# Parts of two feed-forward groups begun inside the attention of batch 0, with norms, key tiles and loads re-ordered

## The chip, the core and the metric

The kernel runs on one core of a Trainium2 chip. The metric is the device time of one execution in microseconds; lower is better. TensorE (PE in the profile) does the matrix products, VectorE (DVE) and ScalarE (ACT) the elementwise work, GpSimd (POOL) the squares and the transfers that cast, SyncE (SP) issues most other transfers.

## The reference

Two stages, one feeding the other. First, cosine attention: 8 batches of 12 heads, 448 positions, head size 64. Then a feed-forward layer on 3584 tokens: 768 to 2048, leaky ReLU with slope 0.01, 2048 to 768.

```python
q_n = q / (np.linalg.norm(q, axis=-1, keepdims=True) + 1e-06)
k_n = k / (np.linalg.norm(k, axis=-1, keepdims=True) + 1e-06)
scores = np.matmul(q_n, k_n.transpose(0, 1, 3, 2)) / tau
scores = scores - np.max(scores, axis=-1, keepdims=True)
attn = np.exp(scores)
attn = attn / (np.sum(attn, axis=-1, keepdims=True) + 1e-09)
x = np.matmul(attn, v)            # then heads side by side: (3584, 768)
h = x @ w_in
out = np.maximum(0.01 * h, h) @ w_out
```

## The kernel before

The order of work on every engine is the order of the program text: the kernel is written under a manual schedule, and each engine and each queue takes its instructions in that order, waiting where an input or a buffer is not ready.

Heads go in pairs: pair `s` (0 to 47) has two heads, six pairs to a batch. Two pairs make a group of four heads, `j` (0 to 23), three groups to a batch. The 448 positions are three tiles of 128 and a rest of 64; the rests of two heads share one tile.

For each pair: `load_qk(s)` brings q and k on SyncE (four transfers: q main, k main, and the two rests); the buffers rotate among four pairs, so a load waits until the pair four before it is normalised and squared. `squares(s)` (L163, GpSimd) and `sums(s)` (L174, VectorE) and `roots(s)` (L181 to 183, ScalarE) and `normalise(s)` (L191 and L195, VectorE) give the normalised heads `qn`. `hold(...)` (L426) is a tiny GpSimd copy that makes GpSimd wait for `qn`. `transposes(s)` turns them: for pairs below 12 on TensorE (L209) with a VectorE copy (L233), from pair 12 on with a transposing transfer on SyncE (L227). `scores(s, ...)` or `key_tiles` gives the score tiles (L252, TensorE) and their exponentials (L264, ScalarE).

For each group: `totals(j)` sums the exponentials with matmuls by ones (L275) and inverts the sum on ScalarE (L286, L287, tile `rb`); `products(j, e)` multiplies with the values (L275): twelve matmuls on `v_b(j)`, then four on the rest tiles `v_rem` of the batch; `scale(j, e)` (L306, VectorE) writes two of the six rows of `xT`. `attend(j)` is all of these for one group. `load_v(j)` and `load_v_rem(b)` bring the values on GpSimd's queue.

Feed-forward: tokens go in chunks `c`, 384 and 512 columns in turn. `first(c, m)` (L324) is one of 16 groups of six matmuls over the six rows of `xT`, with a Prelu on ScalarE (L330); `second(c, ts, half)` (L349) is 16 matmuls over `hT` and one half of `w_out`, with a copy on VectorE (L360) and the store. `load_w_in(i)` brings a quarter of `w_in` (half the columns, every second row), `load_w_out(half)` half the columns of `w_out`, on GpSimd's queue.

Three stages follow each other. (1) A loop over the six pairs of batch 0: attention only; `fill(2)` puts two idle matmuls on a tile `warm` (L417) into TensorE's order where it would wait. (2) Straight code around pairs 6 and 7: group 2, and the first 13 groups `first(0, m)` in hand-written places. (3) A loop over batches 1 to 7 by units; each unit has an attention part, one pair's norms, and as many feed-forward groups from a queue as a plan of costs (`ATTEND`, `BLOCK`) gives it.

Accumulators lie in eight banks. `banks(count, keep)` deals the free bank that has been unused longest; `keep` holds a bank until `given_back`. In stage 1 pairs of banks (scores) come from 0 to 3 and single ones from 4 to 7.

Of the kernel before, what the change touches and what calls it, by code (L numbers as in the profile page):

```python
# [10 lines left out]
AF = mybir.ActivationFunctionType  # L11
# [5 lines left out]
def kernel(  # L17
# [10 lines left out]
    nc = tc.nc  # L28
# [15 lines left out]
    WARM = 22  # L44
    ATTEND = 5500
    BLOCK = 1800
    assert REM == 64 and D == 64

    ctx.enter_context(tc.manual_schedule())
# [23 lines left out]
    kept = {}  # L73
    deals = {"n": 0, "apart": True}

    def banks(count, keep=None):
        lo, hi = (0, 8) if not deals["apart"] else (0, 4) if count == 2 else (4, 8)
        x = min(
            (i for i in range(lo, hi, count) if not set(range(i, i + count)) & set(kept.values())),
            key=lambda i: max(age[i : i + count]),  # L80
        )
        deals["n"] += 1
        age[x : x + count] = [deals["n"]] * count
        if keep:
            kept[keep] = x
        return ps[:, x] if count == 1 else ps[:, x : x + count]

    def given_back(keep):
        deals["n"] += 1
        age[kept.pop(keep)] = deals["n"]  # L90
# [12 lines left out]
    def load_w_in(i):  # L103
        n0, e = i // 2 * (D_ff // 2), i % 2
        gp.dma_start(
            out=w_in_sb[:, e::2, n0 : n0 + D_ff // 2], in_=w_in_r[e, :, :, n0 : n0 + D_ff // 2]
        )

    def load_w_out(half):
        n0 = half * HALF  # L110
        gp.dma_start(out=w_out_sb[:, :, n0 : n0 + HALF], in_=w_out_r[:, :, n0 : n0 + HALF])
# [42 lines left out]
    def squares(s, engs=(gp, gp)):  # L154
        if s >= NSLOT:
            return
        tiles = []
        for x, eng, name in zip(raw[s], engs, ("sq0", "sq1")):
            sq = sqp.tile(list(x.shape), F32, name=name)
            if eng is nc.scalar:  # L160
                nc.scalar.activation(sq, x, func=AF.Square)
            else:
                eng.tensor_tensor(sq, x, x, op=ALU.mult)  # L163
            tiles.append(sq)
        sqs[s] = tiles
# [12 lines left out]
    def roots(s):  # L178
        if s >= NSLOT:
            return  # L180
        nc.scalar.activation(ss[s], ss[s], func=AF.Ln, bias=tiny)  # L181
        nc.scalar.activation(ss[s], ss[s], func=AF.Exp, scale=0.5)
        nc.scalar.activation(ss[s], ss[s], func=AF.Identity, bias=eps)  # L183
# [3 lines left out]
    def normalise(s):  # L187
        if s >= NSLOT:
            return
        r = smp.tile([128, 14], F32, name="r")  # L190
        nc.vector.reciprocal(r, ss[s])  # L191
        qn[s] = qnp.tile([128, 7, 2, D], BF16, name="qn")
        for x, lo, hi, r0 in ((raw[s][0], 0, 4, 0), (raw[s][1], 4, 7, 8)):
            nt = hi - lo
            nc.vector.tensor_tensor(  # L195
                qn[s][:, lo:hi],
                x.rearrange("p h t d -> p t h d"),
                r[:, r0 : r0 + 2 * nt].rearrange("p (h t) -> p t h", h=2)
                .unsqueeze(3).to_broadcast([128, nt, 2, D]),
                op=ALU.mult,  # L200
            )
# [35 lines left out]
    def scores(s, kis):  # L237
        key_tiles([(s, ki) for ki in kis])
# [43 lines left out]
    def totals(j):  # L282
        sm = banks(1)
        strip_products(j, sm, lambda g, ki: ones, lambda g: ones_rem[:, g // 2])
        rb = rbp.tile([128, S], F32, name="rb")
        nc.scalar.activation(rb, sm[:, :S], func=AF.Ln)  # L286
        nc.scalar.activation(rb, rb, func=AF.Exp, scale=-1.0)  # L287
        rbs[j] = rb
# [3 lines left out]
    def products(j, e, po=None):  # L292
        b, jj = divmod(j, NQ)
        if po is None:
            po = banks(1, (j, e))
        pos[j, e] = po
        vm = vb[j].rearrange("p h t (d e) -> p h t e d", e=2)
        vr = vrb[b % 2].rearrange("p j g (d e) -> p j g e d", e=2)
        strip_products(j, po, lambda g, ki: vm[:, g, ki, e], lambda g: vr[:, jj, g, e])
# [15 lines left out]
    def chunk_cols(c):  # L315
        return (0, MAIN) if c % 2 == 0 else (MAIN, 512)

    def first(c, m):
        c0, n = chunk_cols(c)
        if m == 0:  # L320
            hT[c] = htp.tile([128, MT, 512], BF16, name="hT")
        pm = banks(1)
        for kt in range(KT):
            nc.tensor.matmul(  # L324
                out=pm[:, :n],
                lhsT=w_in_sb[:, kt, m * 128 : (m + 1) * 128],
                rhs=xT[c // 2][:, kt, c0 : c0 + n],
                start=(kt == 0), stop=(kt == KT - 1),
            )
        nc.scalar.activation(out=hT[c][:, m, :n], in_=pm[:, :n], func=AF.Prelu, alpha=0.01)  # L330

    osb = {}

# [43 lines left out]
    work = {}  # L377
    for c in range(B):
        c0, n = chunk_cols(c)
        groups = [(KT * n, lambda c=c, m=m: first(c, m)) for m in range(MT)]  # L380
        order = [(ts, half) for half in range(2) for ts in range(n // 128)] if c == 0 else [
            (ts, half) for ts in range(n // 128) for half in range(2)
        ]
        work[c] = groups + [
            (MT * HALF, lambda c=c, ts=ts, half=half: second(c, ts, half)) for ts, half in order
        ]
# [27 lines left out]
    def fill(count):  # L414
        wm = banks(1)
        for i in range(count):
            nc.tensor.matmul(  # L417
                out=wm, lhsT=warm[:, :128], rhs=warm, start=(i == 0), stop=(i == count - 1)
            )
# [34 lines left out]
    for s in range(NPAIR):  # L454
        j = s // 2 - 1 if s >= 2 else None
        even = s % 2 == 0
        n = s + 2 if s + 2 <= NPAIR else None
        scores(s, (0,))
        if s == 1:
            roots(2)  # L460
        if j is not None and not even:
            products(j, 1)
        scores(s, (1,))
        fill(2)
        if s and n:
            sums(n, (0,))
        normalise(s + 1)
        load_qk(s + 5)
        if j is not None and not even:
            scale(j, 0)  # L470
        hold(qn[s + 1][:, 6, 0, 0:1])
        squares(s + 3)
        if not even:
            load_v(s // 2 + 1)
        if s != 1 and s < 5:
            load_w_in(max(s - 1, 0))
        if s == 5:
            load_v_rem(1)
        if n:
            sums(n, (1,))  # L480
        scores(s, (2,))
        if not even:
            fill(2)
            scores(s, (3,))
        transposes(s + 1)
        if s == 0:
            sums(2, (0,))
        if not even:
            fill(2)
        if n and s:  # L490
            roots(n)
        if j is not None and not even:
            scale(j, 1)
        if j is not None and even:
            totals(j)
            products(j, 0)

    def attend(j):
# [4 lines left out]
        for e in range(2):  # L503
            scale(j, e)

    def norms(s):
        roots(s)
        normalise(s)
        if s >= DMA_FROM:
            transposes(s)  # L510
        load_qk(s + 4)


    deals["apart"] = False
    s, j = NPAIR, NQ - 1
# [1 line left out]
    scores(s, (0, 1))  # L517
    sums(s + 1)
    feed_groups(0, 1)
    norms(s + 1)  # L520
    load_w_out(0)
    hold(qn[s + 1][:, 6, 0, 0:1])
    squares(s + 3)
    sums(s + 2)
# [14 lines left out]
    feed_groups(0, 2)  # L539
    scores(s + 1, (1, 2))  # L540
    normalise(s + 3)
    load_qk(s + 7)
    feed_groups(0, 1)
    transposes(s + 2)
    sums(s + 4)
# [1 line left out]
    roots(s + 4)  # L547
    scores(s + 1, (3,))
    normalise(s + 4)
    load_qk(s + 8)  # L550
    hold(qn[s + 4][:, 6, 0, 0:1])
    squares(s + 5)
    feed_groups(0, 1)
# [24 lines left out]
    for b in range(1, B):  # L578
        queue += work[b - 1]
        units = opened if b == 1 else whole  # L580
        costs = [BLOCK + (ATTEND if at is not None else 0) for at, _, _ in units[1:] + [(2, 0, 0)]]
        for i, (at, tiles, ahead) in enumerate(units):
            share = (sum(g[0] for g in queue[:-1]) + sum(costs[i:])) / (len(units) - i) - costs[i]
            if b > 1 and i == 0:
                at = -1
            if at is not None:
                attend(b * NQ + at)
                load_v(b * NQ + at + 2)
            key_tiles([(b * NPAIR + p, ki) for p, ki in tiles])
            done = 0  # L590
            if b == 1 and i < 2:

                if i == 1:
                    cost, fn = queue.pop(0)
                    fn()
                    done += cost
                transposes(NPAIR + 4 + i)
            if ahead and b * NPAIR + ahead < NSLOT:
                s = b * NPAIR + ahead
                sums(s)  # L600
                norms(s)
                hold(qn[s][:, 6, 0, 0:1])
                squares(s + 1)
            if at == 1:
                load_v_rem(b + 1)
            while len(queue) > 1 and (i == len(units) - 1 or done + queue[0][0] / 2 <= share):
                cost, fn = queue.pop(0)
                fn()
                done += cost
# [38 lines left out]
```

## Time and profile before

| | |
|---|---|
| median of 3 runs | 430.74 us (430.70 to 430.92) |
| the profiled execution | 430.73 us |
| its span, first to last instruction | 428.7 us |
| TensorE busy | 417.2 us, 97% of the span |
| ScalarE, VectorE, GpSimd busy | 267.5, 186.5, 137.0 us |
| granted TensorE clock | 0.998 |
| bytes moved | 53.65 MB, mean 125 GB/s |

In the span TensorE does, by groups of instructions: second feed-forward product 151.9 us, first 150.9 us, scores 46.5 us, products and totals 79.7 us, and 15.6 us of warm-up and fill matmuls. Matmuls are pipelined, so a group's time by the timeline is more than what the chain of waits gives it; where a duration is needed to add up, the chain's is used.

Read a timeline line as: start, duration, engine, source line, operation, output <- inputs, shape, count, and in brackets how long the engine sat idle before it and what released it. Read a wait line as: engine and line that waited, what it waited for, microseconds in total, times, longest. In lines on queues the figures are packets, megabytes and share of the 16 engines' time; "DMA to landing" runs from the issue until the data are there.

### The profile page before, as it was taken

What the parts mean: (1) busy time and instruction counts of PE and PEld (TensorE: products, weight loads), DVE (VectorE), ACT (ScalarE), POOL (GpSimd) and SP (SyncE); (2) the same over time, 40 slices, a digit from 0 to 9 for tenths busy, and PEclk for the clock granted to TensorE, in tenths of its full rate; (3) what the DMA queues carried; (4) which work ended last, traced back from release to release, by engine and by line L of the source; (5) the groups of instructions that cost most, each with busy time, mean ns of one, the idle gap of its engine ahead of it and who ended that gap; (6) DMA issues with size and microseconds to landing.
All of it is one profiled execution on the core that took longest, in us unless ns stands there. A gap on an engine that the chain in (4) does not pass through costs nothing.

```text
span 428.7 us, 8667 instructions
## 1 busy us (share of the span) xinstructions
PE 417.2 (97%) x3333; PEld 208.9 (49%) x3333; DVE 186.5 (44%) x366; ACT 267.5 (62%) x494; POOL 137.0 (32%) x208
## 2 busy tenths in 40 slices
PE   8699999999999999999999999999999999999995
PEld 3234554544455555544455555544455555554563
DVE  5775756643453545343353444552444441220021
ACT  4997886677753886577663786658745596434300
POOL 4676542714124143612324132631334110000000
PEclk9999999999999999999999999999999999999999
DMA  7999999964558355953748456865447422010032
GB/s 173 193 230 220 217 224 210 195 166 92 121 120 169 97 120 104 221 100 90 128 98 161 105 127 134 170 105 142 86 99 152 72 64 41 38 73 2 0 75 73
DMA packets 102888, 53.65 MB, mean 125 GB/s; under 512 B 68928, under 2 KB 97856, under 8 KB 102848
## 3 DMA queue, kind: packets, MB, share of 16 engines
q1 hardware_dynamic: 77296, 40.98, 39.1%
q0 software_dynamic: 25056, 11.80, 21.9%
q8 instruction: 26, 0.43, 0.4%
q10 hardware_dynamic: 496, 0.33, 0.2%
q14 instruction: 14, 0.11, 0.1%
HBM read 45.61 MB, written 11.01 MB: 132 GB/s over the span
## 4 chain that ended last, share of the span: by engine, by line
PE 91%; DVE 4%; ACT 1%; DMA 1%; SPq 1%; issue 1%; POOL 1%; DVEq 0%; POOLq 0%
PE ps L324 34%; PE ps L349 33%; PE ps L275 13%; PE ps L252 9%; DVE qn L195 2%; DMA q_h<-in_q_dram 1%; PE ps L209 1%; DVE ss L174 1%; POOL sq L163 1%; PE ps L417 1%; SPq L127 0%; DVE r L191 0%; ACT ss L183 0%; DVE qkT L233 0%; DVE osb L360 0%
## 5 line engine op out<-in xcount | busy, mean ns | idle before, releaser
L349 PE MATMUL ps<-w_out_sb,hT 128*128 128x384 bf16 x896 | 151.9, 326 | 0.2 <-DVE xT L306 0.2
L264 ACT ACTIVATE pe<-ps 128x896 bf16<-128x896 f32 x144 | 122.5, 918 | 46.2 <-PE ps L252 44.5
L324 PE MATMUL ps<-xT,w_in_sb 128*128 128x384 bf16 (+1 forms) x768 | 150.9, 353 | 0.0
L349 PEld LDWEIGHTS <-hT 128*128 128x128 bf16 x896 | 85.3, 98 | 64.1 <-issue 9.6
L324 PEld LDWEIGHTS <-w_in_sb 128*128 128x128 bf16 x768 | 73.1, 98 | 72.4 <-issue 7.0
L330 ACT ACTIVATE hT<-ps 128x384 bf16<-128x384 f32 (+1 forms) x128 | 65.1, 540 | 40.5 <-PE ps L324 40.1
L426 POOL CAST seen<-qn 128x1 f32<-128x1 bf16 x47 | 8.6, 182 | 209.7 <-DVE qn L195 209.7
L360 DVE COPY osb<-ps 128x384 f32<-128x384 f32 (+1 forms) x56 | 30.9, 552 | 99.3 <-PE ps L349 86.9
L174 DVE TENSOR_REDUCE ss<-sq 128x8 f32<-128x512 f32 (+1 forms) x96 | 56.7, 613 | 17.8 <-POOL sq L163 15.7
L252 PE MATMUL ps<-qkT 64*128 64x448 bf16 (+1 forms) x384 | 46.5, 358 | 4.9 <-ACT pe L264 2.9
L163 POOL TENSOR_TENSOR sq<-q_h 128x512 f32<-128x512 f32 x46 | 47.7, 1036 | 2.4 <-DMA q_h<-in_k_dram 1.6
L191 DVE RECIPROCAL r<-ss 128x14 f32<-128x14 f32 x48 | 11.6, 241 | 82.5 <-ACT ss L183 82.5
L306 DVE TENSOR_TENSOR xT<-ps,rb 128x448 bf16<-128x448 f32 x48 | 27.9, 619 | 30.1 <-ACT rb L287 30.1
L163 POOL TENSOR_TENSOR sq<-k_h 128x384 f32<-128x384 f32 x46 | 37.7, 820 | 0.0
L275 PE MATMUL ps<-pe,v_b 128*32 128x448 bf16 x576 | 35.6, 353 | 0.0
L286 ACT ACTIVATE rb<-ps 128x448 f32<-128x448 f32 x24 | 13.0, 541 | 34.5 <-PE ps L275 34.5
L195 DVE TENSOR_TENSOR qn<-q_h,r 128x512 bf16<-128x512 f32 x48 | 33.4, 697 | 1.9 <-DVE r L191 0.3
L252 PEld LDWEIGHTS <-qkT 64*128 64x128 bf16 (+1 forms) x384 | 13.0, 96 | 38.6 <-issue 31.8
L195 DVE TENSOR_TENSOR qn<-k_h,r 128x384 bf16<-128x384 f32 x48 | 26.5, 551 | 0.0
L264 ACT ACTIVATE pr<-ps 128x896 bf16<-128x896 f32 x24 | 22.3, 927 | 0.0
L275 PEld LDWEIGHTS <-v_b 128*32 128x32 bf16 x576 | 15.2, 97 | 11.9 <-issue 0.4
L150 POOL DMA_DIRECT2D v_rem<-in_v_dram x32 | 20.4, 643 | 0.1
(39 smaller groups left out, 183.5 us busy)
## 6 DMA issues: line engine op xcount, KB each, us to landing
q_h<-in_q_dram SPq DMA_DIRECT2D x48, 192.0 KB, 3.2
k_h<-in_k_dram SPq DMA_DIRECT2D x47, 192.0 KB, 3.2
out_dram<-osb SPq DMA_DIRECT2D x30, 192.0 KB, 3.3
v_b<-in_v_dram POOLq DMA_DIRECT2D x24, 192.0 KB, 5.1
out_dram<-osb SPq DMA_DIRECT2D x12, 384.0 KB, 2.9
w_in_sb<-in_moe_w_in_dram POOLq DMA_DIRECT2D x4, 768.0 KB, 9.8
w_out_sb<-in_moe_w_out_dram POOLq DMA_DIRECT2D x2, 1536.0 KB, 21.0
q_h<-in_q_dram SPq DMA_DIRECT2D x48, 32.0 KB, 3.8
```

Of the source, the lines that this page charges most:

```text
L150: gp.dma_start(out=vrb[b % 2][lo : lo + 64, :, g], in_=r[g])
L163: eng.tensor_tensor(sq, x, x, op=ALU.mult)
L174: nc.vector.tensor_reduce(o.rearrange("p (h t) -> p h t", h=2), sqs[s][i], axis=AX.X, op=ALU.add)
L195: nc.vector.tensor_tensor(qn[s][:, lo:hi], x.rearrange("p h t d -> p t h d"), r[:, r0 : r0 + 2 * nt].rearrange("p (h t) -> p t h", h=2) .u ...
L252: nc.tensor.matmul(out=out[:, a, :S], lhsT=x[rows, c0:c1], rhs=x[rows, 0:S], start=True, stop=True,)
L264: nc.scalar.activation(out=dst, in_=sc[:, :, :S], func=AF.Exp, scale=inv_tau)
L275: nc.tensor.matmul(out=x[32 * g : 32 * g + 32, :S], lhsT=weights(g, ki) if ki < 3 else rem(g), rhs=pe[s][:, ki, a, :] if ki < 3 else pr[j] ...
L306: nc.vector.tensor_tensor(xT[m][:, 2 * jj + e, half * S : (half + 1) * S], pos.pop((j, e))[:, :S], rbs[j], op=ALU.mult,)
L324: nc.tensor.matmul(out=pm[:, :n], lhsT=w_in_sb[:, kt, m * 128 : (m + 1) * 128], rhs=xT[c // 2][:, kt, c0 : c0 + n], start=(kt == 0), stop= ...
L330: nc.scalar.activation(out=hT[c][:, m, :n], in_=pm[:, :n], func=AF.Prelu, alpha=0.01)
L349: nc.tensor.matmul(out=po2[:, :HALF], lhsT=hT[c][:, m, ts * 128 : (ts + 1) * 128], rhs=w_out_sb[:, m, half * HALF : (half + 1) * HALF], st ...
L360: nc.vector.tensor_copy(out=o[:, half * HALF : half * HALF + cut], in_=po2[:, :cut])
```

## The change

Seven edits:

- In pair 5 of stage 1 the last two of three fills are replaced by the first four of the six matmuls of `first(0, 0)` and of `first(0, 1)`; the remaining two of each stay at the old place. Banks 4 and 5 are kept for them until their Prelu. For this `scale(1, 1)` goes ahead of them.
- `scores(3, (0,))` and `scores(5, (0,))` move from the start of their pairs to the end of the pair before, between `totals` and `products`.
- `load_w_in(1)` moves from pair 2 to pair 1 (behind `load_v(1)`).
- `load_w_out(0)` moves from stage 2 (behind the norms of pair 7) to pair 5, ahead of `load_v(3)` and `load_v_rem(1)` on GpSimd's queue.
- The loads of pairs 13 and 14 leave stage 2; in stage 3 each step's load is of pair `s + 2` for pairs 11 and 12, of 15 and 16 for pair 13, and of `s + 3` after that, where it was `s + 4`.
- In stage 3 `sums(s)` and `roots(s)` come ahead of what the first two units of batch 1 put before the norms (one feed-forward group, the transposes); `normalise(s)` and the rest stay behind it.
- `norms` is taken apart into its calls.

```diff
     BLOCK = 1800
+    SOON = 2
...
-    def banks(count, keep=None):
+    def banks(count, keep=None, which=None):
-        x = min(
+        x = which if which is not None else min(
...
-    def first(c, m):
+    pms = {}
+
+    def first(c, m, kts=range(KT)):
+
         c0, n = chunk_cols(c)
-        if m == 0:
+        if c not in hT:
             hT[c] = htp.tile([128, MT, 512], BF16, name="hT")
-        pm = banks(1)
-        for kt in range(KT):
+        if (c, m) not in pms:
+            pms[c, m] = banks(1)
+        pm = pms[c, m]
+        for kt in kts:
...
-        nc.scalar.activation(out=hT[c][:, m, :n], in_=pm[:, :n], func=AF.Prelu, alpha=0.01)
+        if kts[-1] == KT - 1:
+            nc.scalar.activation(
+                out=hT[c][:, m, :n], in_=pms.pop((c, m))[:, :n], func=AF.Prelu, alpha=0.01
+            )
+            if (c, m, 0) in kept:
+                given_back((c, m, 0))
...
-        groups = [(KT * n, lambda c=c, m=m: first(c, m)) for m in range(MT)]
+        groups = [
+            (KT * n, lambda c=c, m=m: first(c, m, range(KT - 2 if c == 0 and m < SOON else 0, KT)))
+            for m in range(MT)
+        ]
...
-        scores(s, (0,))
+        if s != 3 and s != 5:
+            scores(s, (0,))
...
         squares(s + 3)
+        if s == 5:
+            load_w_out(0)
         if not even:
             load_v(s // 2 + 1)
-        if s != 1 and s < 5:
-            load_w_in(max(s - 1, 0))
+        if s != 2 and s < 5:
+            load_w_in(s - s // 3)
         if s == 5:
             load_v_rem(1)
...
         scores(s, (2,))
+        if s == 5:
+
+            scale(j, 1)
+            for m in range(SOON):
+                pms[0, m] = banks(1, (0, m, 0), 4 + m)
+            first(0, 0, range(KT - 2))
+        elif not even:
+            fill(2)
         if not even:
-            fill(2)
             scores(s, (3,))
         transposes(s + 1)
         if s == 0:
             sums(2, (0,))
-        if not even:
+        if s == 5:
+            first(0, 1, range(KT - 2))
+        elif not even:
             fill(2)
         if n and s:
             roots(n)
-        if j is not None and not even:
+        if j is not None and not even and s < 5:
             scale(j, 1)
         if j is not None and even:
             totals(j)
+            scores(s + 1, (0,))
             products(j, 0)
...
-    norms(s + 1)
-    load_w_out(0)
+    roots(s + 1)
+    normalise(s + 1)
+    load_qk(s + 5)
...
-    load_qk(s + 7)
...
-    load_qk(s + 8)
...
             done = 0
+            s = b * NPAIR + ahead if ahead else NSLOT
+            if s < NSLOT:
+                sums(s)
+                roots(s)
             if b == 1 and i < 2:
...
-            if ahead and b * NPAIR + ahead < NSLOT:
-                s = b * NPAIR + ahead
-                sums(s)
-                norms(s)
+            if s < NSLOT:
+                normalise(s)
+                if s >= DMA_FROM:
+                    transposes(s)
+
+                for n in (s + 2,) if s <= NPAIR + 6 else (s + 2, s + 3) if s == NPAIR + 7 else (s + 3,):
+                    load_qk(n)
                 hold(qn[s][:, 6, 0, 0:1])
                 squares(s + 1)
```

More of the change, by code (lines that the diff above doesn't have):

```diff
@@ L504, in attend @@
             scale(j, e)
[L506 to L511, printed above, removed]
     deals["apart"] = False
```

## The prediction

> **What bounds the kernel now.** I read the busy shares and the chain first, then TensorE's waits, then TensorE, ScalarE, VectorE and GpSimd in order of time between 20 and 85 us, and last the DMA queues in short windows.
>
> ```profile
> PE 417.2 (97%) x3333; PEld 208.9 (49%) x3333; DVE 186.5 (44%) x366; ACT 267.5 (62%) x494; POOL 137.0 (32%) x208
> PE 91%; DVE 4%; ACT 1%; DMA 1%; SPq 1%; issue 1%; POOL 1%; DVEq 0%; POOLq 0%
> PE ps L252 <- DVE osb L360: 0.7, 1, 0.7
> PE ps L349 <- DVE xT L306: 0.2, 1, 0.2
> ...
> 34.32 0.61 PE L417 MATMUL ps<-warm 128*128 128x512 bf16 x2
> 35.58 0.59 PE L417 MATMUL ps<-warm 128*128 128x512 bf16 x2
> 36.10 0.75 PE L275 MATMUL ps<-pe,ones 128*32 128x448 bf16 x12
> 38.97 4.07 PE L324 MATMUL ps<-xT,w_in_sb 128*128 128x384 bf16 x24
> 42.88 0.76 PE L209 MATMUL ps<-id,qn 128*128 128x128 bf16 x7
> 55.50 0.74 PE L275 MATMUL ps<-pe,v_b 128*32 128x448 bf16 x12
> 56.06 0.36 PE L275 MATMUL ps<-pr,v_rem 128*32 128x448 bf16 x4
> ```
>
> TensorE is the bound. From about 29.6 us to the end it stops once only, 0.88 us near 75 us (the last two waits above). So whatever is removed from its order before that is time, if nothing it then meets is late; and whatever makes it wait there is time too. The last two lines are the first products of pair group 3 (batch 1): they read v_b(3) and then v_rem of batch 1.
>
> ```profile
> 34.65 1.03 POOL L163 TENSOR_TENSOR sq<-q_h 128x512 f32<-128x512 f32 x1 [1.14 <-DMA q_h<-in_k_dram]
> 36.42 0.81 POOL L142 DMA_DIRECT2D v_b<-in_v_dram  x1
> 37.23 2.48 POOL L150 DMA_DIRECT2D v_rem<-in_v_dram  x4
> 39.70 1.21 POOL L111 DMA_DIRECT2D w_out_sb<-in_moe_w_out_dram  x1
> ...
> L142 POOL DMA_DIRECT2D v_b<-in_v_dram x1: 826/826/826, 48.8 to 48.8; - x1
> DMA to landing us min/median/max: 12.3/12.3/12.3
> L111 POOL DMA_DIRECT2D w_out_sb<-in_moe_w_out_dram x1: 1208/1208/1208, 39.7 to 39.7; - x1
> DMA to landing us min/median/max: 19.1/19.1/19.1
> ...
> q0 software_dynamic: 321, 0.25, 78.2%
> q1 hardware_dynamic: 319, 0.22, 45.7%
> ```
>
> GpSimd's transfers share queue q0, and they land in the order of issue: the w_out half issued at 39.70 lands at 58.8 (39.7 + 19.1), and v_b(4), issued at 48.80, takes 12.3 us, landing at 61.1, 2.3 behind it, where the one issued at 76.47 takes 4.9. The last two lines (52 to 54 us) show q0 and the SyncE queue q1 taking turns packet by packet: 321 against 319. In the same way I worked out the landings before it: w_in's fourth part 43.2 (32.1 + 11.1), v_b(3) 45.4 (36.4 + 9.0), the last v_rem 47.0 (39.1 + 7.9).
>
> **The change part by part.**
>
> *Two fills replaced.* The fills at 34.32 and 35.58 hold 0.54 and 0.43 us of the chain: 0.97 off TensorE's order. In their places come twice four matmuls of the first two groups, 8 x 0.167 (24 take 4.01 in the chain) = 1.34 us, taken out after 38.97. Their inputs: the second scale of group 1 moves ahead of the transpose copy on VectorE and ends near 34.28, TensorE arrives at 34.32; w_in's second part had landed at 31.9. Both in time, the scale by 0.04; late, it would cost 0 to 0.6 (one scale is 0.61). But the totals of group 2 (36.10) now start 1.34 - 0.97 = 0.37 later, and behind them hangs a chain that TensorE meets again: totals, ScalarE's rb, the two exponentials at 38.89, the Prelu of group 0, the roots of pair 7, reciprocal and normalise (42.08 to 43.24), transposes of pair 7. In the trace of before those transposes already wait: 7 take 0.56 elsewhere, 0.76 here, and the chain has the last three start at 43.30. After, TensorE would reach them at 43.05 - 0.97 = 42.08 and their last three could start at 43.67. So the 0.97 turns into idle time and the next group starts 0.37 later than before. Bounds: -0.97 (chain not binding) and +0.37; I take +0.37, since the wait is in the trace already. The banks kept for the two groups make TensorE wait for nothing it did not wait for.
>
> *First key tiles of pairs 3 and 5 ahead of the products.* Two matmuls (0.29) change places with 16 (0.87). ScalarE idles 0.51 and 0.49 before these exponentials (24.21, 33.06) and gets that back, but TensorE has no gap from 20.8 to 27.3 nor from 29.7 to 38.9, so nothing on the path: 0. Cover: pair 5's qkT copy ends at 31.08 and TensorE arrives at 31.12; if late, at most one copy, 0 to 0.6.
>
> *w_in's second part one pair earlier.* Its issue (0.81 on GpSimd) moves from 23.28 to about 20.65, ahead of the hold at 21.31, which slips 0.15 and with it squares, sums and normalise of the next pairs; transposes at 26.33 still find qn (24.6) done. On q0 it could start only behind v_b(1), whose packets run to about 24.4, where it started near 24.8: the queue gains 0 to 0.8, I take 0.4.
>
> *w_out's first half ahead of v_b(3) and v_rem.* This decides. It is now issued at 36.42 on GpSimd, v_b(3) at 37.6, v_rem to 40.9; no GpSimd work is due before 43.38, so the issuing costs nothing. On q0 the half needs 58.8 - 47.0 = 11.8 us behind what precedes it. After: 43.2 - 0.4 + 11.8 = 54.6; v_b(3) 2.3 behind it, 56.9; then the v_rem, 768 packets of 128 B, which took 47.0 - 45.4 = 1.6 with q1 nearly empty, and would take 3.5 at the pace that q0 has beside a busy q1 (some 110 packets per half us near 57). q1 holds pair loads then, so 1.6 to 3.5; I take 2.5: 59.4. The earliest is 58.4 (the same bytes had landed by 58.8, less 0.4); the latest 61.4 (the half in 12.8, its 2048 packets at the 321 in 2 us above, and v_rem in 3.5). TensorE, 0.37 late, wants v_b(3) at 55.9 and v_rem at 56.4. It stops twice, about 1.0 and 2.4 us, and everything behind it (products, key tiles of pair 8, all later groups) moves by 59.4 - 56.06 = 3.3 us against before (2.3 to 5.3); the 0.37 is inside that, and a gain before it would be too.
>
> The Trainium skill (page "DMA: Bandwidth & Descriptors", section "Anatomy of one DMA — SWDGE (gpsimd) path") fits such a transfer as 2.0 us plus its bytes over 436 GB/s; 1.57 MB would take an estimated 5.6 us, v_b(3) and v_rem would then be there in time, and the sum would be that of the first rival below. The row of 11.8 us decides against it, because q1 shares the engines.
>
> *Batch 1's norms: sums and roots ahead of the group and the transposes, normalise behind.* In before, pair 12's sums stand behind an output copy and a transpose copy (64.70 to 65.7); its reciprocal is at 67.80. With sums at 64.65 and roots at 65.8, normalise begins near 66.8, 1.0 earlier, and hence squares, sums and normalise of pair 13; the copy at 74.29 and the scale at 74.76, which hold TensorE, come 0.5 to 1.0 earlier than 74.37 and 74.84. TensorE wants them at 74.2 and 74.55. The 0.88 goes, all of it shifted by the 3.3: -0.88 (bounds 0 and -0.88).
>
> *Pair loads.* SyncE runs ahead of the text: load 13 still waits only for its buffer and goes at 49.74. Load 14 (55.14) now stands behind pair 12's DMA transpose, load 15 (62.06) behind pair 13's, and so on, three pairs ahead instead of four. A load landed 4.4 to 5.6 us after issue at 71 us; load 14 would then land within about 1.5 us of its squares (74.71). q0 is empty by then, since fewer loads stand beside w_out's second half. I cost it 0; without that cover, up to 1.5, between 77 and 82 us. Later the distance is some 13 us for 3 us of transfer: 0.
>
> *Sum*, against the profiled execution (430.73 us: span 428.7 and 2.0 around it; the median of three runs is 430.74): 430.73 + 3.3 - 0.88 = 433.2.
>
> **The rivals.**
> 1. *Values in time: not slower.* If the v_rem land by 56.4 instead of 59.4, TensorE does not stop, and 430.73 + 0.37 - 0.88 = 430.2. For it: alone, q0 moved 0.37 MB in 2 us (26 to 28 us), which would make the half 8.5 us. Against it: pair loads 11 to 13 are on q1 from 47 us on in before, and their issue hangs on normalise, which is not earlier.
> 2. *Half clock.* The granted clock fell to 0.50 about 2.6 us after the last matmul (424.15 to 426.7), and the first fills ran at 634 ns against 379 for some 4.8 us. If one of the two stops exceeds 2.6 us, up to 4.8 us run at half speed, up to 2.4 more, say 2.0: 435.2. Against it: stops of 1.0 and 2.4 with matmuls between. The Trainium skill ("TensorE: Matmul & The Clock Gate", "What's actually happening") has the clock halved after an idle window of about 3.4 us, which these stops would not fill.
> 3. *Everything works.* Values in time and the pair 7 chain not binding: 430.73 - 0.97 - 0.88 = 428.9. Against it, both waits as read above.
>
> **How the numbers follow.** Forecast 0.70, rival 1 0.15, rival 2 0.10, rival 3 0.05. The forecast's own range is 432.1 (2.3 - 0.88) to 435.1 (5.3 - 0.88). With rival 1 taken in, 430.0 to 435.1 leaves out rival 3, half of rival 2 and the forecast's edges, 2 in 10. A change of 0.2%, 0.86 us, is about what runs of this kernel can tell from none. Slower: the forecast and rival 2, 0.80; rival 1 lies 0.12% below before, so two thirds of it are the same, 0.10; faster 0.10.
>
> **What would show it.** TensorE's waits should hold a new line, products waiting for v_b and v_rem, 2.3 to 5.3 us near 56; w_out's half landing near 54.6, the v_rem near 59.4; transposes of pair 7 waiting about 1 us near 43; the two waits near 75 gone; ScalarE's two half-us gaps gone. I am wrong if the v_rem land before 56.5, or if their wait stays and later work makes it up, for which the trace of before has only the 0.88.

## The result and the profile after

The changed kernel takes 433.0 us (median of 6 runs, 432.46 to 435.1) against 430.83 us for the kernel before (6 runs beside it, 430.68 to 430.98): a ratio of 1.0057, 95% interval 1.0038 to 1.0076. It is slower, by 2.2 us. The forecast was 433.2.

The profiled execution is the slowest of these runs, 435.1 us with a span of 433.2, so its trace accounts for 4.4 us more than the profiled execution of before (430.73), not for 2.2. The line numbers of the changed kernel differ: L276 are totals and products, L253 key tiles, L210 transposes, L330 and L360 the two feed-forward products, L431 the fills.

From the page of the changed kernel, the chain that ended last. TensorE is busy 97% of the span as before, but the chain now holds transfers, which before were 1% of it:

```profile
PE 85%; DMA 8%; POOL 3%; SPq 1%; DVE 1%; ACT 0%; issue 0%; POOLq 0%; DVEq 0%
```

TensorE has new waits in it: 1.2 us in total for `v_b`, 0.8 for `v_rem`, 0.7 for `qn` and 0.7 for `xT`. The two near 75 us of the kernel before (for the output copy and for a scale) are gone. TensorE in order of time; the brackets hold the new waits:

```profile
34.80 0.81 PE L330 MATMUL ps<-xT,w_in_sb 128*128 128x384 bf16 x4 [0.54 <-DVE xT L307]
37.00 0.75 PE L276 MATMUL ps<-pe,ones 128*32 128x448 bf16 x12
43.73 0.81 PE L210 MATMUL ps<-id,qn 128*128 128x128 bf16 x7 [0.75 <-DVE qn L196]
44.38 2.11 PE L330 MATMUL ps<-xT,w_in_sb 128*128 128x384 bf16 x12
...
57.75 0.75 PE L276 MATMUL ps<-pe,v_b 128*32 128x448 bf16 x12 [1.18 <-DMA v_b<-in_v_dram]
59.07 0.36 PE L276 MATMUL ps<-pr,v_rem 128*32 128x448 bf16 x1 [0.28 <-DMA v_rem<-in_v_dram]
59.91 0.74 PE L276 MATMUL ps<-pr,v_rem 128*32 128x448 bf16 x2 [0.47 <-DMA v_rem<-in_v_dram]
60.25 1.52 PE L276 MATMUL ps<-pe,v_b 128*32 128x448 bf16 x12
63.95 3.09 PE L330 MATMUL ps<-xT,w_in_sb 128*128 128x384 bf16 x18
...
79.23 0.74 PE L253 MATMUL ps<-qkT 64*128 64x448 bf16 x6
82.61 0.68 PE L253 MATMUL ps<-qkT 64*128 64x448 bf16 x6
```

The same places in the kernel before, as far as the prediction does not show them:

```profile
43.48 2.11 PE L324 MATMUL ps<-xT,w_in_sb 128*128 128x384 bf16 x12
56.25 0.74 PE L275 MATMUL ps<-pe,v_b 128*32 128x448 bf16 x12
58.19 3.09 PE L324 MATMUL ps<-xT,w_in_sb 128*128 128x384 bf16 x18
...
73.47 0.74 PE L252 MATMUL ps<-qkT 64*128 64x448 bf16 x5
78.12 0.68 PE L252 MATMUL ps<-qkT 64*128 64x448 bf16 x6
```

The starts set side by side give the account of the profiled execution. The first groups after pair 7's transposes start 0.9 us later (44.38 against 43.48). The second products of group 3 start 4.0 us later (60.25 against 56.25), which contains the 0.9. The next feed-forward group starts 5.8 us later (63.95 against 58.19): 1.8 us more, although nothing waits there, because twelve matmuls that took 0.74 now take 1.52. Here the clock is at half, as shown below. Then 1.3 us come back between pair 11's two sets of key tiles (3.38 us from 79.23 to 82.61; 4.65 us from 73.47 to 78.12 before), and 4.5 us remain to the end.

The transfers, with the issue in the first line of each pair and the time to landing in the second: the half of `w_out` lands at 55.6 (35.9 + 19.7), `v_b(3)` at 57.7 (37.2 + 20.5) and the last `v_rem` at 60.2 (39.8 + 20.4; the four took 20.5, 20.5, 20.7 and 20.4).

```profile
L112 POOL DMA_DIRECT2D w_out_sb<-in_moe_w_out_dram x1: 1223/1223/1223, 35.9 to 35.9; - x1
DMA to landing us min/median/max: 19.7/19.7/19.7
...
L143 POOL DMA_DIRECT2D v_b<-in_v_dram x1: 762/762/762, 37.2 to 37.2; - x1
DMA to landing us min/median/max: 20.5/20.5/20.5
...
L151 POOL DMA_DIRECT2D v_rem<-in_v_dram x4: 628/636/646, 37.9 to 39.8; - x4
DMA to landing us min/median/max: 20.4/20.5/20.7
```

And the 1.8 us: each line below is a stretch of the changed kernel (from:to, then its length and the busy time of each engine), and the last three columns are the granted clock, the transfers' share and GB/s. A mean of 0.72 between 60 and 61, and of 0.57 between 63 and 64, puts the fall to half at about 60.4 and the return at about 63.9.

```profile
57.00:60.00 3.00, 1.50 (x15) 0.51 (x15) 0.00 (x0) 0.74 (x2) 1.83 (x3) 1.00 1.35 212
60.00:61.00 1.00, 1.00 (x13) 0.46 (x16) 0.25 (x1) 0.00 (x0) 0.00 (x0) 0.72 1.32 202
61.00:63.00 2.00, 2.00 (x19) 0.43 (x7) 1.20 (x3) 0.31 (x1) 0.00 (x0) 0.50 1.32 206
63.00:64.00 1.00, 1.00 (x10) 0.70 (x9) 0.85 (x2) 1.00 (x2) 0.00 (x0) 0.57 1.30 203
```

### The profile page after: what moved, and what is told of

The parts are those of the page before. It is cut to its first block, busy times and chain, and to the rows that moved or that the text cites. A ratio compares the mean times of both kernels' runs of the same rounds, so it can differ in the third digit from the quotient of the medians.

```text
span 433.2 us, 8650 instructions
## 1 busy us (share of the span) xinstructions
PE 418.9 (97%) x3329; PEld 209.0 (48%) x3329; DVE 188.4 (43%) x366; ACT 267.7 (62%) x494; POOL 138.1 (32%) x208
## 4 chain that ended last, share of the span: by engine, by line
PE 85%; DMA 8%; POOL 3%; SPq 1%; DVE 1%; ACT 0%; issue 0%; POOLq 0%; DVEq 0%
PE ps L360 34%; PE ps L330 31%; PE ps L276 12%; PE ps L253 8%; DMA v_rem<-in_v_dram 5%; DMA q_h<-in_k_dram 3%; POOL sq L164 1%; DMA q_h<-in_q_dram 1%; SPq L128 1%; DVE qn L196 1%; POOL v_b L143 0%; POOL v_rem L151 0%; POOL w_out_sb L112 0%; PE ps L210 0%; SPq L125 0%
## 5 line engine op out<-in xcount | busy, mean ns | idle before, releaser
L330 PE MATMUL ps<-xT,w_in_sb 128*128 128x384 bf16 (+1 forms) x768 | 151.4, 353 | 0.7 <-DVE xT L307 0.7
L360 PE MATMUL ps<-w_out_sb,hT 128*128 128x384 bf16 x896 | 151.9, 326 | 0.0
L360 PEld LDWEIGHTS <-hT 128*128 128x128 bf16 x896 | 85.2, 98 | 62.9 <-issue 8.0
L330 PEld LDWEIGHTS <-w_in_sb 128*128 128x128 bf16 x768 | 73.1, 98 | 73.1 <-issue 8.1
L253 PE MATMUL ps<-qkT 64*128 64x448 bf16 (+1 forms) x384 | 46.7, 362 | 4.2 <-ACT pe L265 2.9
L164 POOL TENSOR_TENSOR sq<-k_h 128x384 f32<-128x384 f32 x46 | 38.7, 842 | 0.0
L276 PE MATMUL ps<-pe,v_b 128*32 128x448 bf16 x576 | 36.4, 357 | 1.2 <-DMA v_b<-in_v_dram 1.2
L253 PEld LDWEIGHTS <-qkT 64*128 64x128 bf16 (+1 forms) x384 | 13.0, 96 | 39.0 <-issue 32.7
L196 DVE TENSOR_TENSOR qn<-k_h,r 128x384 bf16<-128x384 f32 x48 | 27.7, 578 | 0.0
L276 PEld LDWEIGHTS <-v_b 128*32 128x32 bf16 x576 | 15.2, 97 | 13.4 <-DMA v_b<-in_v_dram 1.6
L151 POOL DMA_DIRECT2D v_rem<-in_v_dram x32 | 20.4, 646 | 0.1
```

The source lines that it names most:

```text
L151: gp.dma_start(out=vrb[b % 2][lo : lo + 64, :, g], in_=r[g])
L196: nc.vector.tensor_tensor(qn[s][:, lo:hi], x.rearrange("p h t d -> p t h d"), r[:, r0 : r0 + 2 * nt].rearrange("p (h t) -> p t h", h=2) .u ...
L253: nc.tensor.matmul(out=out[:, a, :S], lhsT=x[rows, c0:c1], rhs=x[rows, 0:S], start=True, stop=True,)
L276: nc.tensor.matmul(out=x[32 * g : 32 * g + 32, :S], lhsT=weights(g, ki) if ki < 3 else rem(g), rhs=pe[s][:, ki, a, :] if ki < 3 else pr[j] ...
L330: nc.tensor.matmul(out=pm[:, :n], lhsT=w_in_sb[:, kt, m * 128 : (m + 1) * 128], rhs=xT[c // 2][:, kt, c0 : c0 + n], start=(kt == 0), stop= ...
L360: nc.tensor.matmul(out=po2[:, :HALF], lhsT=hT[c][:, m, ts * 128 : (ts + 1) * 128], rhs=w_out_sb[:, m, half * HALF : (half + 1) * HALF], st ...
```

## The experiments

The theory: the values of batch 1 land late because the half of `w_out` stands ahead of them on GpSimd's queue; the parts in place of fills give nothing because pair 7's chain binds; the split norms give about 1.3 us; and the clock adds to the stop. The first four kernels take single edits out or in; they ran beside the kernel before at 430.79 us (23 runs).

### Values first

The changed kernel with one order undone:

```diff
-        if s == 5:
-            load_w_out(0)
         if not even:
             load_v(s // 2 + 1)
...
         if s == 5:
             load_v_rem(1)
+            load_w_out(0)
```

> The changed kernel with one line moved: in pair 5 GpSimd issues v_b(3) and v_rem of batch 1 first and the half of w_out behind them, as in the kernel before; all else stays changed. Theory (the values land late because the half stands ahead of them on GpSimd's queue): the products of group 3 no longer wait, v_b(3) lands near 46 and v_rem near 48, the granted clock near 60 us stays at 1.0, and what is left is 0.9 lost up to pair 7's transposes and 1.3 gained near 75 us in the traces: 430.4 us (429.9 to 430.9). Rival (the loss is made by the other edits, the pair loads or the parts of the two groups): 432.5 or more. Rival (the stop only moves to the first second-product, which then waits for the half): a wait for w_out_sb of over 1 us near 62.

Measured: 430.61 us (11 runs, 430.13 to 430.89), ratio 0.9994 (0.9985 to 1.0003). The products of group 3 run without a stop. In the trace of this kernel:

```profile
56.57 0.74 PE L276 MATMUL ps<-pe,v_b 128*32 128x448 bf16 x12
57.13 0.36 PE L276 MATMUL ps<-pr,v_rem 128*32 128x448 bf16 x4
```

The 2.4 us that this takes off the median of the changed kernel are the price of the order. The half of `w_out`, then last in the queue, is still not waited for. What is left cancels: about 1.1 lost by 55.80, where the totals of group 3 start (54.73 before), and 1.3 gained near 75 us.

### The half first, alone

The kernel before with the same line moved: `load_w_out(0)` goes from behind the norms of pair 7 to pair 5, ahead of `load_v`.

```diff
+        if s == 5:
+            load_w_out(0)
         if not even:
             load_v(s // 2 + 1)
...
     norms(s + 1)
-    load_w_out(0)
```

> The kernel before with one line moved: the half of w_out is issued in pair 5 ahead of v_b(3) and v_rem of batch 1. Theory: v_b(3) lands near 57.5, v_rem near 60, the products of group 3 stop for about 3.5 to 4 us in all against before, the 0.88 near 75 us stays or shrinks a little: 434.2 us (433.0 to 436.0), the upper part where the clock falls to half behind the stop, which costs up to 1.7. Rival (the half by itself is hidden, the loss needs the other edits too): 430.7, or 431.7 at most.

Measured: 437.35 us (4 runs, 436.26 to 438.43), ratio 1.0152 (1.0136 to 1.0168). This edit alone is slower than the whole change, and it cost over a microsecond more than the upper end that I gave. The profiled run is the slowest, 438.43 us. The stop for `v_b` is one piece here, and the clock falls in it, at about 58.5, and comes back at about 65.4 (0.82 between 65 and 66):

```profile
59.77 1.31 PE L275 MATMUL ps<-pe,v_b 128*32 128x448 bf16 x12 [3.68 <-DMA v_b<-in_v_dram]
...
58.00:59.00 1.00, 0.00 (x0) 0.00 (x0) 0.00 (x0) 0.00 (x0) 1.00 (x2) 0.77 1.34 242
59.00:60.00 1.00, 0.23 (x4) 0.14 (x8) 0.00 (x0) 0.00 (x0) 0.05 (x1) 0.50 1.38 203
60.00:62.00 2.00, 1.96 (x15) 0.51 (x7) 0.00 (x0) 0.00 (x0) 0.00 (x0) 0.50 1.29 214
62.00:64.00 2.00, 1.97 (x18) 0.60 (x17) 0.62 (x1) 0.00 (x0) 0.00 (x0) 0.50 1.24 234
64.00:65.00 1.00, 1.00 (x9) 0.29 (x6) 0.55 (x1) 0.03 (x1) 0.00 (x0) 0.50 1.27 214
65.00:66.00 1.00, 1.00 (x12) 0.50 (x9) 0.08 (x1) 1.00 (x2) 0.00 (x0) 0.82 1.30 192
```

The twelve matmuls at 59.77 take 1.10 us to the next start, where they took 0.56 before, and from the second products (62.37) to the next feed-forward group (65.91) it is 3.54 us instead of 1.94. So the half clock cost 2.1 us in this run, where I had allowed 1.7. The larger part of the overshoot is the transfers: `v_b(3)` landed at 59.7 (39.0 + 20.7) and the last `v_rem` at 62.4 (41.6 + 20.8), where I had expected 57.5 and 60. The queue was late already ahead of the moved transfer: the fourth part of `w_in` landed at 45.3 (32.6 + 12.7), against 43.2 in the kernel before, with the same program up to there. Why it was late in this run is not shown.

### The norms, alone

The kernel before with the split norms of the unit loop and nothing else (loads as before, four pairs ahead):

```diff
             done = 0
+            s = b * NPAIR + ahead if ahead else NSLOT
+            if s < NSLOT:
+                sums(s)
+                roots(s)
...
-            if ahead and b * NPAIR + ahead < NSLOT:
-                s = b * NPAIR + ahead
-                sums(s)
-                norms(s)
+            if s < NSLOT:
+                normalise(s)
+                if s >= DMA_FROM:
+                    transposes(s)
+                load_qk(s + 4)
```

> The kernel before with the norms of the unit loop alone changed: sums and roots ahead of the group and transposes of batch 1's first two units, normalise behind; all loads as before. Theory (the two waits near 75 us hang on VectorE's late sums of pairs 12 and 13, and nothing behind them was waiting): they are gone, 429.5 us (429.3 to 429.9), since the traces show 1.3 less between pair 11's first key tile and its third. Rival (the wait moves to the next late thing, within the following units): 430.5 to 430.9.

Measured: 429.59 us (7 runs, 429.17 to 431.32), ratio 0.9974 (0.9963 to 0.9985). The gain is real, 1.2 us. The rival has a part in it: in the slowest run, the profiled one, the gain is used up by the next late thing, the second half of `w_out` (issued at 50.6, landed 25.3 us later):

```profile
75.98 2.77 PE L349 MATMUL ps<-w_out_sb,hT 128*128 128x384 bf16 x16 [1.50 <-DMA w_out_sb<-in_moe_w_out_dram]
```

In before this half landed at 72.5 (49.6 + 22.9), 2.9 us ahead of the product that reads it (75.43). The split norms bring that product 1.3 forward, and in this run the half also came 3.4 later.

### The parts, alone

The kernel before with the first four matmuls of `first(0, 0)` and `first(0, 1)` in place of two fills of pair 5, as in the change (banks 4 and 5 kept, the second scale of group 1 ahead of them):

```diff
+        if s == 5:
+            scale(j, 1)
+            for m in range(SOON):
+                pms[0, m] = banks(1, (0, m, 0), 4 + m)
+            first(0, 0, range(KT - 2))
+        elif not even:
+            fill(2)
...
+        if s == 5:
+            first(0, 1, range(KT - 2))
+        elif not even:
             fill(2)
```

> The kernel before with the parts of the two groups alone: two fills of pair 5 replaced by four matmuls of each of the first two groups, the second scale of group 1 moved ahead of them, banks kept. Theory (the chain of totals 2, rb, exponentials, roots and normalise of pair 7 binds, so that every later start of totals 2 is lost at pair 7's transposes): they wait about 1 us, and the time is 430.8 + 0.4 = 431.2, up to 431.7 where the scale is late as in the changed kernel. Rival (the fills removed are a gain): 429.8.

Measured: 431.17 us (11 runs, 431.03 to 431.75), ratio 1.0010 (1.0001 to 1.0018): about 0.4 us slower, as the chain of pair 7 says. Its trace has that wait, and the scale in time (the first part at 34.23 without a wait):

```profile
36.45 0.75 PE L276 MATMUL ps<-pe,ones 128*32 128x448 bf16 x12
43.18 0.81 PE L210 MATMUL ps<-id,qn 128*128 128x128 bf16 x7 [0.75 <-DVE qn L196]
```

The second four kernels ran beside the kernel before at 430.74 us (17 runs).

### Neither the half first, nor the parts, nor w_in early

The changed kernel with values first, `load_w_in` at its old places and the fills back. What stays are the norms, the later pair loads and the key tiles ahead of the products.

```diff
-    SOON = 2
+    SOON = 0
...
-        if s == 5:
-            load_w_out(0)
...
-        if s != 2 and s < 5:
-            load_w_in(s - s // 3)
+        if s != 1 and s < 5:
+            load_w_in(max(s - 1, 0))
         if s == 5:
             load_v_rem(1)
+            load_w_out(0)
...
-        if s == 5:
-            first(0, 1, range(KT - 2))
-        elif not even:
+        if not even:
             fill(2)
```

> The changed kernel with three of its edits undone: values ahead of the half of w_out again, w_in's second part in pair 2 again, and the fills of pair 5 back in place of the parts. What stays: key tiles of pairs 3 and 5 ahead, norms split, pair loads later. Theory (the norms are the whole gain, and the later pair loads keep the second half of w_out in time, for which the run with the norms alone waited 1.5 us in its slowest run): 429.5 us (429.3 to 429.8), no wait for w_out_sb. Rival (the later pair loads give nothing): 429.6 with the same spread of 2 us. Rival (the key tiles ahead are a gain of their own, 0.5 each): 428.6.

Measured: 429.51 us (7 runs, 429.17 to 429.65), ratio 0.9970 (0.9959 to 0.9981). The median is that of the norms alone, so the key tiles ahead give nothing that can be measured. The runs lie within 0.5 us where the norms alone had 2.1: with the pair loads later, the second half of `w_out` landed at 70.5 (50.9 + 19.6) in the profiled run instead of 75.9, and nothing waited for it. That this narrows the spread rests on 7 runs each.

### Values first, w_in back

The kernel of the first experiment with `load_w_in` at its old places.

> The changed kernel with values ahead of the half, and w_in's second part issued in pair 2 again. Theory (w_in's earlier part holds up pair 7's load, GpSimd's squares of pair 7 then overlap VectorE's normalise of pair 6, whose second instruction takes 1.17 instead of 0.55, and the scale ahead of the first part ends 0.5 to 0.65 late): the wait for xT near 35 us falls from 0.65 to 0.1 or less, totals 2 start about 0.4 later than in before instead of 0.9, 430.1 us (429.8 to 430.4). Rival (the scale is late by itself): wait unchanged, 430.6.

Measured: 429.85 us (11 runs, 429.48 to 430.08), ratio 0.9979 (0.9970 to 0.9988). It is 0.76 us below the first experiment. There GpSimd waits 0.9 us for a load of pair 7, and its squares then run beside VectorE's normalise of pair 6, both longer than elsewhere; here they do not. The kept traces of the other two kernels with `w_in` early, the changed one and the one of the next experiment, show the same wait (0.79 and 0.92 us) and the same long pair of instructions; no kept trace without that edit does at this place. GpSimd and VectorE first with `w_in` early, then VectorE with it back:

```profile
31.17 1.03 POOL L164 TENSOR_TENSOR sq<-q_h 128x512 f32<-128x512 f32 x1 [0.91 <-DMA q_h<-in_k_dram]
32.17 1.27 POOL L164 TENSOR_TENSOR sq<-k_h 128x384 f32<-128x384 f32 x1
32.68 1.18 DVE L196 TENSOR_TENSOR qn<-k_h,r 128x384 bf16<-128x384 f32 x1
33.78 1.14 DVE L307 TENSOR_TENSOR xT<-ps,rb 128x448 bf16<-128x448 f32 x2
```

```profile
32.81 0.55 DVE L196 TENSOR_TENSOR qn<-k_h,r 128x384 bf16<-128x384 f32 x1
33.28 1.14 DVE L307 TENSOR_TENSOR xT<-ps,rb 128x448 bf16<-128x448 f32 x2
```

So `w_in` one pair earlier, which I had counted as a gain of 0.4 on the queue, costs 0.5 to 0.8.

### Fills in the wait

The changed kernel with TensorE kept busy where it waits for the values:

```diff
     def attend(j):
         totals(j)
+        if j == NQ:
+            fill(8)
         po = banks(2)
```

> The changed kernel with eight idle matmuls on the warm tile (8 x 0.22 = 1.7 us) between totals and products of group 3, where TensorE waits for v_b(3). Theory (the stop lets the granted clock fall to half in some runs, which makes the changed kernel's spread of 432.5 to 435.1): the granted clock stays at 1.0 between 58 and 66 us, the median is 432.7 (432.3 to 433.3) and the runs lie within 1 us. Rival (the spread comes from when the transfers land, not from the clock): median 433.0 to 433.5 and the same spread. Rival (the fills overrun the landing): 433.5 or more.

Measured: 433.06 us (5 runs, 432.94 to 433.83), ratio 1.0058 (1.0045 to 1.0071). The clock is at 1.0 between 55 and 66 us in its trace, and the runs lie within 0.9 us, where those of the changed kernel had 2.6. But the median is that of the changed kernel and lies in the range of the theory and of the first rival. In this run `v_b(3)` landed at 57.1 (37.7 + 19.4) and the fills ended at 58.9; the last `v_rem` landed at 59.6 (40.3 + 19.3), and the second products start at 59.67. So it is the landing of `v_rem` that set the time here, and the fills cost next to nothing.

For the other runs of the changed kernel only the mean granted clock is on record. It is 0.999 in those of 432.68 and 433.18 us, which leaves room for little more than 1 us at half clock; the profiled run, with 3.4 us of it, has 0.995. So the median of 433.0 does not need the half clock, and the slowest run does.

### The half first, with fills

The same question where the stop is long: the kernel of the second experiment with `fill(16)` at that place. It ran beside the kernel before at 430.9 us (9 runs), and so did the last kernel of this section.

> The kernel before with the half of w_out ahead of the values (437.35 us), with 16 idle matmuls on the warm tile (3.5 us) where TensorE waits 3.7 us for v_b(3). Theory (what that run lost beyond the wait is the clock, at half for some 6 us behind the stop): the granted clock stays at 1.0 between 56 and 70 us and the time falls by 2 to 3, to 434.3 to 435.3. Rival (the loss is all transfers that land late): 437 or more, since the fills change no transfer.

Measured: 434.62 us (4 runs, 434.52 to 435.46), ratio 1.0093 (1.0079 to 1.0106). The median is 2.7 us lower, as the theory had it. The granted clock of the profiled run stays at 1.0:

```profile
55.00:60.00 5.00, 5.00 (x48) 2.15 (x44) 1.05 (x3) 1.73 (x4) 2.78 (x4) 1.00 1.44 209
60.00:65.00 5.00, 5.00 (x55) 2.63 (x44) 3.11 (x6) 3.58 (x7) 0.00 (x0) 1.00 1.25 222
```

Not all of the 2.7 need be the clock. The fills change no transfer, yet in this profiled run `v_b(3)` landed at 57.3 (37.4 + 19.9) and the last `v_rem` at 59.8 (40.0 + 19.8), over 2 us earlier than in the profiled run of the second experiment. Between these two runs, which differ by 3.9 us, the second products start 2.3 earlier (60.04 against 62.37), mostly by the landings, and from there to the next feed-forward group it takes 1.94 us (60.04 to 61.98) instead of 3.54: at least 1.6 are the clock. How the 2.7 between the medians divide is not shown.

### Pair 7's norms early

The kernel with values first and `w_in` back, and the chain that makes pair 7's transposes wait taken out of the way of the parts: its sums in pair 5 on VectorE, its roots ahead of group 2's totals on ScalarE, its normalise between group 2's products and scales.

```diff
             scores(s, (3,))
+        if s == 5:
+            sums(7)
         transposes(s + 1)
...
-    def attend(j):
+    def attend(j, between=lambda: None):
         totals(j)
         po = banks(2)
         for e in range(2):
             products(j, e, po[:, e])
+        between()
...
-    attend(j)
+    roots(s + 1)
+    attend(j, lambda: normalise(s + 1))
+    load_qk(s + 5)
     scores(s, (0, 1))
-    sums(s + 1)
     feed_groups(0, 1)
-    roots(s + 1)
-    normalise(s + 1)
-    load_qk(s + 5)
```

> As the changed kernel with values first and w_in's second part in pair 2, and pair 7's norms early: its sums on VectorE in pair 5 ahead of pair 6's transpose copy, its roots ahead of group 2's totals on ScalarE, its normalise between group 2's products and scales. Theory (pair 7's chain of sums, roots, normalise behind the exponentials is what turned the removed fills into a wait): pair 7's transposes no longer wait, the 0.97 of fills becomes time, 428.9 us (428.5 to 429.4). Rival (the next late thing takes its place, the scales of group 2 behind the normalise): a wait for xT of about 1 us near 40 us, 429.8 to 430.2.

Measured: 428.57 us (5 runs, 428.35 to 428.84), ratio 0.9951 (0.9939 to 0.9964). This is faster than both kernels, 2.2 us below before and 4.4 below the change. Against the kernel with neither the half first nor the parts (429.51 us, beside the same kernel before) it is 0.94 less, where the two fills hold 0.97. Pair 7's norms early without the parts were not run, so what they give alone is not separated. Pair 7's transposes start at once:

```profile
40.01 2.60 PE L330 MATMUL ps<-xT,w_in_sb 128*128 128x384 bf16 x15 [0.18 <-DVE xT L307]
42.45 0.55 PE L210 MATMUL ps<-id,qn 128*128 128x128 bf16 x7
42.84 2.11 PE L330 MATMUL ps<-xT,w_in_sb 128*128 128x384 bf16 x12
```

### Four buffers for the exponentials

That kernel with four buffers instead of three:

```diff
-    pep = ctx.enter_context(tc.tile_pool(name="pe", bufs=3))
+    pep = ctx.enter_context(tc.tile_pool(name="pe", bufs=4))
```

> The kernel with pair 7's norms early (428.57 us), with four buffers for the exponentials (pe) instead of three. Theory (the key tiles moved ahead of the products gave ScalarE nothing, since the exponentials of pairs 3 and 5 write the buffer that the products of the group before still read; not TensorE's order but the buffer held them): ScalarE's two waits of 0.5 us before pe near 24 and 33 us, released by the products' matmuls, are gone or below 0.1; the time moves by less than 0.3, since TensorE has no gap there: 428.3 to 428.7. Rival (they wait for the scores themselves): both waits stay. Rival (ScalarE's gain reaches pair 4's key tiles near 29 us): 428.0.

Measured: 428.79 us (5 runs, 428.31 to 429.09), ratio 0.9950 (0.9937 to 0.9964): the same time. With three buffers ScalarE still waits for the products, in spite of the key tiles ahead of them; with four it does not, and waits 0.25 for the second key tile instead. First three buffers, then four:

```profile
33.15 2.54 ACT L265 ACTIVATE pe<-ps 128x896 bf16<-128x896 f32 x3 [0.50 <-PE ps L276]
```

```profile
32.59 0.90 ACT L265 ACTIVATE pe<-ps 128x896 bf16<-128x896 f32 x1
33.74 1.75 ACT L265 ACTIVATE pe<-ps 128x896 bf16<-128x896 f32 x2 [0.25 <-PE ps L253]
```

## Why the prediction was right, and where it was not

**The half ahead of the values: right, and it decides.** Landings were forecast at 54.6, 56.9 and 59.4, and came at 55.6, 57.7 and 60.2 in the profiled execution. The order alone accounts for 2.4 us between the medians of the changed kernel and the one with values first. The half took 12.3 us behind `w_in`'s fourth part (43.3 to 55.6), where I took 11.8. The Trainium skill (page "DMA: Bandwidth & Descriptors", section "Anatomy of one DMA — SWDGE (gpsimd) path") fits such a transfer as 2.0 us plus its bytes over 436 GB/s, an estimated 5.6 us for the half; the 12.3 us measured beside a busy second queue do not agree. The Trainium skill (page "DMA: Bandwidth & Descriptors", section "Two DMAs through the same engine are not ordered") says that within one queue of one DMA engine descriptors start in order. The three landings, which come in the order of issue, agree with that.

**The delay at group 3: right in kind, mis-sized.** Forecast 3.3, measured 4.0 in the profiled execution, inside the bounds of 2.3 to 5.3. The last landing came 0.8 later than forecast: 0.5 because `w_in`'s fourth part landed at 43.3 and not at 42.8, 0.5 because the half took 12.3, less 0.2 for `v_b(3)`, 2.1 behind it where I took 2.3. The 2.5 for the `v_rem` (57.7 to 60.2) came out as taken.

**The clock: rival 2 came true in the profiled run, and its condition was wrong.** I required one stop of more than 2.6 us. The listed waits are 1.18, 0.28 and 0.47, and the clock still fell, for 3.4 us at a cost of 1.7. Without that the profiled run would be at 433.4. Two runs, of 432.68 and 433.18 us, show by their mean clock that they did without such a fall, so a time near the median does not need it.

**The norms: right, with a term too small.** I took 0.88 from the idle times of the two waits; the starts before and after give 1.3, and the kernel with the norms alone 1.2. The ends of matmuls are modelled, so a stop measured between starts is safer than one read from the idle column.

**The parts in place of fills: right.** +0.37 was forecast for them, the parts alone cost 0.4, and the kernel that has both the parts and pair 7's chain out of the way is 0.94 faster than the one with neither. In the changed kernel itself the loss at that place was 0.9, since the scale came 0.54 late. I had put its margin at 0.04 and bounded it by 0.6, but not connected it with `w_in`.

**`w_in` one pair earlier: wrong.** The step said that the queue gains 0.4. The fourth part of `w_in` was issued later, at 33.2 instead of 32.1, because GpSimd waited for pair 7's load; it landed at 43.3, where it had landed at 43.2. What I costed was GpSimd's issue time and the queue; what the earlier transfer took came from SyncE's loads. The last two transfers of pair 7's load, issued near 22, took 8.6 and 9.1 us to land in the changed kernel, where they had taken 5.3 and 5.8; with `w_in` back they took 5.1 and 5.6. Through GpSimd's squares that reached VectorE.

**The key tiles ahead: the cost of nothing was right, the reason half wrong.** I wrote that ScalarE gets its half microseconds back. It does not: those exponentials write the buffer that the products still read, as the run with four buffers shows.

**The pair loads: right.** Cost 0 was taken; the squares of pair 15 do wait 1.79 us for a load near 86.5, and TensorE does not stop behind them. The earlier landing of `w_out`'s second half was foreseen (69.0 against 72.5); that the gain by the norms needs it, as in the slowest run of the norms alone, was not.

The forecast of 433.2 is closer to 433.0 than its terms deserve, and that is luck: in the profiled run 0.7 too little at group 3 and 0.4 too little gain near 75 us nearly cancel. The run at the median has no trace, so its terms are not known.

## What to carry to other kernels

A transfer that is moved earlier on a queue moves everything behind it later: look up who needs those first, and add up the queue by landings, not by sizes. Work taken off the bounding engine is time only as far as the next chain that it meets; when that chain already waits a little before the change, move it along with the work, which made a loss of 0.4 us a gain of 0.9 here. A stop costs more than its length where the clock falls behind it: 1.7 us in the profiled run of the changed kernel, 2.1 in that of the half first. And the same transfer can land 2 us apart in runs with the same order of work up to it, so compare the landings before comparing two profiled runs.

## What the runs showed of the hardware

TensorE's granted clock fell to 0.50 about 2.4 us after the last matmul in the half-first kernel's stop (56.1 to 58.5). In the changed kernel it fell at 60.4, though the 3.4 us before held the 16 short matmuls of the first products and no listed wait above 1.18 us. It stayed there for 3.4 us in the changed kernel and for 6.8, twice that, in the half-first one. With idle matmuls in the stop it stayed at 1.0. The Trainium skill (page "TensorE: Matmul & The Clock Gate", section "What's actually happening") has it fall after an idle window of about 3.4 us and rise after as much activity. The lengths at half, 3.4 and 6.8 us, fit such a window; the fall in the changed kernel does not fit the rule, since no 3.4 us there were idle.

GpSimd's squares and VectorE's normalise, run at the same time, both took longer in the changed kernel: 1.26 us instead of 0.82, and 1.17 instead of 0.55. The other two kernels with the same overlap show 1.27 and 1.18, and 1.26 and 1.18.

The same transfer lands at different times in different runs with the same order of work up to it: the fourth part of `w_in` at 43.2 in the kernel before, at 45.3 with the half first, and at 42.9 (32.2 + 10.7) with the half first and fills.
